# A weight block loaded earlier and multiplied ahead of a pair, at the DMA-bound start of an attention and expert kernel

## The chip, the cores and the metric

The kernel runs on 1 core of one Trainium2 chip. The metric is device microseconds (us) of one execution, as the median of several runs. A profile comes from one of these runs. Its span is about 1.8 us shorter than the run's device time. All times inside a profile count from the start of its span.

Engines: PE is TensorE (PEld its weight loads), DVE is VectorE, ACT is ScalarE, POOL is GpSimd, SP is SyncE.

## The reference, cut to what matters

```python
q, k, v: (batch 8, heads 8, sequence 576, head size 64), float32;  w_in: (512, 2048);  w_out: (2048, 512)

kv  = einsum('bhsd,bhse->bhde', k, v)              # linear attention: one 64x64 matrix per head
out = einsum('bhsd,bhde->bhse', q, kv)
out = out / sqrt(mean(out * out, axis=-1) + 1e-6) * g_norm
x   = out.transpose(0, 2, 1, 3).reshape(4608, 512)
h   = x @ w_in
g   = h * (1 / (1 + exp(-1.702 * h)))
result = g @ w_out                                 # (4608, 512) float32
```

## The kernel before

Batch by batch, the attention part makes x (transposed, float16), and the dense part multiplies it by w_in, gates it and multiplies it by w_out. The eight heads are handled as four pairs, and the 512 rows of w_in as four row blocks of 128. All transfers that matter here are issued by GpSimd one after another and cast from float32 to float16 on the way. The first batch has nothing to hide behind: its k, q, v and the whole of w_in arrive while PE already wants them.

The order of the transfers at the start:

```python
    for c in range(1, NPAIR):            # pairs 1 to 3 of batch 0
        for n in "qkv":
            early_load(n, 0, c, c + 1)
    load_w_in(0, 4, 0, 2)                # w_in: columns 0 to 3 (blocks of 128), row blocks 0 and 1
    load_w_in(0, 4, 2, KO)               # the same columns, row blocks 2 and 3
    load_w_in(4, GROUP)                  # columns 4 and 5, all rows
    load_w_in(GROUP, 10)
    load_w_in(10, FO)
```

PE's program for batch 0 up to the gates:

```python
    for _ in range(3):                   # warm-up: float32 products of zeros
        nc.tensor.matmul(idle_ps, zeros[:, 0:P], zeros, start=True, stop=True)
    a0.q(0)
    busy(2)                              # products that only keep PE busy
    a0.kv(0)
    ...                                  # [cut: pairs 1 and 2 in the same manner]
    a0.q(3)
    a0.kv(3)                             # waits for v of pair 3
    a0.sums(2)
    a0.apply(1)
    a0.out(3)
    a0.rs(2)
    a0.apply(2)
    busy(1)
    d0 = Hidden(0)
    for fo in range(4):                  # row block 0 (ko = 0) of columns 0 to 3
        d0.mm(0, fo, *((ps_h, "hT") if fo < 3 else (ps_a, "att")))
        if fo == 2:
            a0.ss(3)
            a0.apply(3)
    for ko in range(1, KO):
        for fo in range(4):
            d0.mm(ko, fo)
    for fo in range(4, GROUP):
        for ko in range(KO):
            d0.mm(ko, fo, ps_o, "o")
    for fo in range(GROUP):
        d0.gate(fo)
```

Afterwards column blocks 6 to 15 follow (four products and a gate each), then the 64 products with w_out. The work on batch 1 hangs on the numbers of those 64 steps (`at2(27, ...)` means after step 27).

Of the kernel before, what the change touches and what calls it, by code (L numbers as in the profile page):

```python
# [8 lines left out]
F32 = mybir.dt.float32  # L9
# [3 lines left out]
P = 128  # L13
# [3 lines left out]
def kernel(  # L17
# [10 lines left out]
    nc = tc.nc  # L28
# [119 lines left out]
    g_row = const.tile([1, D], F32)  # L148
    nc.scalar.dma_start(out=g_row, in_=g_norm.unsqueeze(0))
    nc.vector.memset(ident, 0.0)  # L150
    zeros = const.tile([P, SM], F32)
    nc.vector.memset(zeros, 0.0)
    nc.vector.memset(kvb[1], 0.0)
    nc.gpsimd.affine_select(  # L154
        out=ident,
# [19 lines left out]
    for c in range(1, NPAIR):  # L175
        for n in "qkv":
            early_load(n, 0, c, c + 1)
    load_w_in(0, 4, 0, 2)
    load_w_in(0, 4, 2, KO)
    load_w_in(4, GROUP)  # L180
    load_w_in(GROUP, 10)
    load_w_in(10, FO)

    nc.scalar.preload_act_table_set("natural_log_exp_and_others")
    nc.vector.memset(eps_t, EPS)
# [261 lines left out]
    def dense(t, units1, units2, group, deep, hid=None):  # L447
        hid = hid or Hidden(t)
        gT = hid.gT
        if group and t:  # L450
            order = [(ko, fo) for part in (range(4), range(4, group)) for ko in (0, 1) for fo in part]
            order += [(ko, fo) for ko in range(2, KO) for fo in range(group)]
            for ko, fo in order:
                pool = (ps_h, "hT") if fo < 3 else (ps_a, "att") if fo == 3 else (ps_o, "o")
                hid.mm(ko, fo, *pool)
            for fo in range(group):
                hid.gate(fo)
        for fo in range(FO):
            if fo >= group:
                for ko in range(KO):  # L460
                    hid.mm(ko, fo)
                hid.gate(fo)
            for u in units1.get(fo, ()):
                u()

        osb = osbs[t] = opool.tile([P, 4, DM], F32, name="osb", tag="osb")
        os = {}

        def project(mo, fo):
            if fo == 0:  # L470
                pool, tag = (ps_h, "hT") if deep and mo < 2 else (ps_o, "o")
                os[mo] = pool.tile([P, DM], F32, name="o", tag=tag)
            nc.tensor.matmul(  # L473
                os[mo],
                gT[:, fo, mo * P : (mo + 1) * P],
                w_out_sb[:, fo, :],
                start=(fo == 0),
                stop=(fo == FO - 1),
            )
            if fo == FO - 1:  # L480
                by_act = mo % 2 if deep or t == B else 0 < t < B - 1 and mo < 2
                copy = nc.scalar.copy if by_act else nc.vector.tensor_copy
                copy(osb[:, mo, :], os[mo])  # L483
                if t == B:
                    store_rest(mo, 0, DM)
                elif t in HALVED and mo % 2:
                    store(t, mo - 1, mo + 1)

        def store_rest(mo, n0, n1):
            for g in range(2):  # L490
                rows = out[(2 * mo + g) * S : (2 * mo + g + 1) * S, n0:n1]
                if 2 * mo + g < EARLY:
                    p0 = SM % PE_
                    rows = rows[bass.DynSlice(NJ * p0 + SM // PE_, R, step=NJ), :]
                else:
                    rows = rows[SM:S, :]
                queue = (nc.sync, nc.scalar)[g]
                queue.dma_start(out=rows, in_=osb[g * R : (g + 1) * R, mo, n0:n1])


        def project_last(mo):
            for i, (n0, n1) in enumerate(LAST):
                o = ps_a.tile([P, n1 - n0], F32, name="oh", tag="att")
                for fo in range(FO):
                    nc.tensor.matmul(  # L505
                        o,
                        gT[:, fo, mo * P : (mo + 1) * P],
                        w_out_sb[:, fo, n0:n1],
                        start=(fo == 0),
                        stop=(fo == FO - 1),  # L510
                    )
                copy = nc.vector.tensor_copy if i else nc.scalar.copy
                copy(osb[:, mo, n0:n1], o)
                store_rest(mo, n0, n1)

        if deep:
            steps = [(mo, 4 * i + k) for i in range(3) for mo in range(4) for k in range(4)]
            steps += [(mo, f + k) for f in (12, 14) for mo in range(2) for k in range(2)]
            steps += [(mo, 12 + k) for mo in (2, 3) for k in range(4)]
        else:  # L520
            steps = [(mo, fo) for mo in range(4 - (t == B)) for fo in range(FO)]
        for n, (mo, fo) in enumerate(steps):
            project(mo, fo)
            for u in units2.get(n, ()):
                u()
        if t == B:
            project_last(3)
        if t < EARLY:

            n = 0  # L530
            while n < SM:
                mo, j, p = n // P, n // PE_, n % PE_
                m = min((mo + 1) * P, (j + 1) * PE_) - n
                nc.sync.dma_start(
                    out=out[t * S : (t + 1) * S, :][bass.DynSlice(NJ * p + j, m, step=NJ), :],
                    in_=osb[n % P : n % P + m, mo, :],
                )
                n += m
        elif t < B and t not in HALVED:
            store(t, 0, J)  # L540
# [25 lines left out]
            )  # L566


    for _ in range(3):
        nc.tensor.matmul(idle_ps, zeros[:, 0:P], zeros, start=True, stop=True)  # L570
    a0.q(0)
    busy(2)
    a0.kv(0)
# [16 lines left out]
    a0.out(2)  # L590
    a0.rs(1)
    a0.q(3)
    a0.kv(3)
    a0.sums(2)
    a0.apply(1)
    a0.out(3)
    a0.rs(2)
    a0.apply(2)
    busy(1)
    d0 = Hidden(0)  # L600
    for fo in range(4):
        d0.mm(0, fo, *((ps_h, "hT") if fo < 3 else (ps_a, "att")))
        if fo == 2:
            a0.ss(3)
            a0.apply(3)
    for ko in range(1, KO):
        for fo in range(4):
            d0.mm(ko, fo)
    for fo in range(4, GROUP):
        for ko in range(KO):  # L610
            d0.mm(ko, fo, ps_o, "o")
    for fo in range(GROUP):
        d0.gate(fo)
    load_w_out(0, 4)
    early_load("q", 1, 0, NPAIR)
    load_w_out(4, 8)
    for c in (0, 2):
        load_half("k", 1, c, c + 2)
        load_half("v", 1, c, c + 2)
        if c == 0:  # L620
            load_w_out(8, 12)
        else:
            load_w_out(12, 14)
            load_w_out(14, FO)
    load_q(2, nc.gpsimd)

    nc.gpsimd.dma_start(out=g_all, in_=g_norm.unsqueeze(0).to_broadcast([P, D]))
# [8 lines left out]
    for t in range(NT):  # L636
# [12 lines left out]
        if t == 0:  # L649
            at1(7, of(0, "out", NPAIR))  # L650
            at2(4, setattr, a0, "ss_pool", Attention.ss_pool)
            at2(4, of(0, "ss", NPAIR, True))
            at2(4, of(0, "apply", NPAIR))
            at1(8, start, 1)
            for l in range(2):
                r = slice(l * PH, (l + 1) * PH)
                at1(8, nc.vector.memset, kpad[r, :, :, (1 - l) * D : (2 - l) * D], 0.0)
            for c in range(NPAIR):
                at1(12, of(1, "pack_q", c))
                at2(9 + 3 * c, of(1, "q", c))  # L660
                at2((21, 21, 33, 33)[c], of(1, "pack_k", c))
                at2((27, 28, 42, 43)[c], of(1, "kv", c))
                o = (32, 35, 50, 53)[c]
                at2(o, of(1, "out", c))
                if c == NPAIR - 1:
                    at2(46, load_kv, 2)
                at2((38, 46, 56, 59)[c], of(1, "ss", c))
                at2((38, 46, 56, 59)[c], of(1, "apply", c))
        elif b < B:
            if t == 1:  # L670
                at2(46, setattr, live[1], "ss_pool", Attention.ss_pool)
                at2(46, of(1, "out", NPAIR))
                at2(53, of(1, "ss", NPAIR))
                at2(53, of(1, "apply", NPAIR))
            f0 = 5 if t == 1 else 2
            at1(f0, cast_q, b)
            at1(f0, start, b)
            at1(f0, of(b, "transpose_q"))
            if t + 2 < B:
                at1(f0, load_q, t + 2)  # L680
                at1((10 if t == 1 else 9) + 4, load_kv, t + 2)
            for c in range(NPAIR):
                at1(f0, of(b, "pack_k", c))
                at1((10 if t == 1 else 9) + c, of(b, "kv", c))
            at2(6, nc.scalar.preload_act_table_set, "natural_log_exp_and_others")
            for j in range(J):
                at2((1, 4, 8, 11)[j], of(b, "rows", j))
            at2(7, of(b, "turn", 0))
            at2(16, of(b, "turn", 2))
            at2(27, of(b, "out", NPAIR))  # L690
            at2(36, of(b, "ss", NPAIR))
            at2(36, of(b, "apply", NPAIR))
# [31 lines left out]
```

## Time and profile before

| what | value |
|---|---|
| median of the runs beside the changed kernel | 286.96 us (286.64 to 287.28, 6 runs) |
| the profiled run | 286.75 us, span 285.0 us |
| v of pair 3 landed, its product starts | 12.88, 13.02 us |
| w_in row blocks 2 and 3 landed, first product with them | 16.53, 16.58 us |
| column blocks 6 and on start | 20.17 us |
| first product with w_out starts | 29.00 us |
| row block 1 of the dense part starts | 46.83 us |
| last product of the kernel starts | 281.32 us |

The last rows serve as milestones: the first product with w_out tells how the start went, row block 1 what was lost between, the last product the whole.

The page of this profile says three more things: how full DMA was in each fortieth of the span, how many instruction fetches ran, and what the chain that ended last is made of.

```profile
DMA  8999999999589356953798279925401410011022
...
q8 instruction: 13, 0.21, 0.3%
...
PE 93%; DMA 3%; POOL 3%; issue 0%; DVE 0%
```

The first row has a digit for every 7.1 us, in tenths of busy time of 16 engines: DMA is full for the first 70 us (8 or 9 tenths in each of the first ten). The second is queue, packets, MB and share: 13 packets of 16 KB in the queue that the profile calls instruction; the prediction takes them for the fetches of PE's program. They take 0.3% of DMA's time. The third: the end is set by PE for 93% of the span.

### The profile page before, as it was taken

How to read it: one execution, taken by the hardware profiler on the slowest of the kernel's cores; microseconds unless marked ns; L12 is line 12 of the kernel's file. 1: busy time of each engine (PE TensorE's matmuls, PEld its weight loads, DVE VectorE, ACT ScalarE, POOL GpSimd, SP SyncE). 2: the span in 40 equal slices, each digit the busy share in tenths (PEclk: the TensorE clock that was granted, in tenths of full speed). 3: DMA queues.
4: the chain of work that ended last, by engine and by line, in shares of the span. 5: the costliest groups of instructions: out<-in, count | busy, mean ns of one | idle time of the engine just before them, and what ended most of it. 6: DMA issues, size and time to landing. Idle time of an engine off the chain costs nothing.

```text
span 285.0 us, 4335 instructions
## 1 busy us (share of the span) xinstructions
PE 278.8 (98%) x1707; PEld 134.9 (47%) x1707; DVE 119.2 (42%) x231; ACT 156.2 (55%) x273; POOL 57.2 (20%) x82
## 2 busy tenths in 40 slices
PE   7899999999999999999999999999999999999995
PEld 3444554455445544554455445544454444444443
DVE  2650566527661657157713852286327400110001
ACT  2697439766575645574468536763666365016400
POOL 8931551111211121112011401130002100000000
PEclk9999999999999999999999999999999999999999
DMA  8999999999589356953798279925401410011022
GB/s 176 198 207 204 207 246 235 201 240 179 122 165 254 61 145 161 245 85 71 218 200 152 38 215 198 188 39 184 83 2 37 119 65 2 0 67 80 2 74 74
DMA packets 54070, 38.76 MB, mean 136 GB/s; under 512 B 31219, under 2 KB 50931, under 8 KB 53923
## 3 DMA queue, kind: packets, MB, share of 16 engines
q0 software_dynamic: 14960, 15.58, 33.5%
q1 hardware_dynamic: 38688, 22.39, 30.6%
q10 hardware_dynamic: 402, 0.52, 0.6%
q8 instruction: 13, 0.21, 0.3%
q14 instruction: 7, 0.05, 0.1%
HBM read 36.73 MB, written 9.44 MB: 162 GB/s over the span
## 4 chain that ended last, share of the span: by engine, by line
PE 93%; DMA 3%; POOL 3%; issue 0%; DVE 0%
PE hT L436 43%; PE o L473 42%; DMA w_in_sb<-in_moe_w_in_dram 3%; PE kvp L225 3%; PE outR L289 2%; PE oh L505 1%; POOL qraw L91 1%; POOL kraw L91 1%; POOL vbuf L91 1%; PE ss L337 1%; PE q L414 0%; PE outT L268 0%; PE outT L257 0%; POOL w_in_sb L168 0%; POOL ident L154 0%
## 5 line engine op out<-in xcount | busy, mean ns | idle before, releaser
L473 PE MATMUL o<-w_out_sb,gT 128*128 128x512 f16 x560 | 130.7, 379 | 0.0
L445 ACT ACTIVATE gT<-hT 128x512 f16<-128x512 f32 x144 | 84.7, 599 | 76.8 <-PE hT L436 76.5
L436 PE MATMUL hT<-xT,w_in_sb 128*128 128x512 f16 x512 | 116.5, 379 | 0.1
L436 PEld LDWEIGHTS <-w_in_sb 128*128 128x128 f16 x576 | 54.3, 98 | 63.1 <-DMA w_in_sb<-in_moe_w_in_dram 1.6
L473 PEld LDWEIGHTS <-gT 128*128 128x128 f16 x560 | 52.9, 98 | 56.4
L483 DVE COPY osb<-o 128x512 f32<-128x512 f32 x20 | 13.8, 690 | 62.3 <-PE o L473 62.3
L321 POOL TENSOR_TENSOR x<-xr,g_all 128x512 f16<-128x512 f32 x12 | 15.3, 1272 | 71.2 <-DVE xr L314 47.2
L216 DVE COPY kpad<-kraw 64x576 f16<-64x576 f16 x56 | 25.0, 446 | 1.7 <-DMA kraw<-in_k_dram 0.4
L300 DVE TENSOR_REDUCE sum<-sq 128x8 f32<-128x512 f16 x24 | 15.8, 679 | 19.9 <-ACT sq L297 19.9
L238 DVE CAST kvb<-kvp 64x128 f16<-64x128 f32 x28 | 8.1, 288 | 36.5 <-PE kvp L225 36.3
L314 DVE TENSOR_TENSOR xr<-outR,sum 128x512 f32<-128x512 f32 x24 | 15.5, 686 | 11.1 <-ACT sum L311 11.1
L112 POOL DMA_DIRECT2D kraw<-in_k_dram x16 | 10.0, 625 | 48.2 <-DVE kpad L216 42.3
L112 POOL DMA_DIRECT2D vbuf<-in_v_dram x16 | 9.7, 610 | 34.1 <-PE kvp L225 29.3
L321 DVE TENSOR_TENSOR x<-xr,g_all 128x512 f16<-128x512 f32 x12 | 15.2, 1267 | 0.7
L297 ACT ACTIVATE sq<-outR 128x512 f16<-128x512 f32 x24 | 13.6, 591 | 2.0 <-PE outR L289 1.6
L225 PEld LDWEIGHTS <-kpad 128*128 128x128 f16 x252 | 11.1, 98 | 6.5 <-DVE kpad L216 0.2
L436 PE MATMUL hT<-x_rem,w_in_sb 128*128 128x512 f16 x64 | 14.0, 379 | 0.0
L277 ACT ACTIVATE sq<-outT 128x512 f16<-128x512 f32 (+1 forms) x16 | 7.7, 481 | 11.0 <-PE outT L257 9.5
L483 ACT COPY osb<-o 128x512 f32<-128x512 f32 x15 | 8.7, 582 | 6.3 <-PE o L473 6.3
L310 ACT ACTIVATE sum<-sum,eps_t 128x16 f32<-128x16 f32 x12 | 3.7, 308 | 15.0 <-DVE sum L300 14.9
L225 PE MATMUL kvp<-vbuf,kpad 128*128 128x64 f16 x252 | 11.9, 193 | 0.0
L339 ACT ACTIVATE ln<-ss,eps_t 128x512 f32<-128x512 f32 (+1 forms) x16 | 9.4, 585 | 3.4 <-PE ss L337 3.4
(65 smaller groups left out, 140.7 us busy)
## 6 DMA issues: line engine op xcount, KB each, us to landing
qf<-in_q_dram SPq DMA_DIRECT2D x5, 1024.0 KB, 8.7
out_dram<-osb SPq DMA_DIRECT2D x10, 512.0 KB, 2.9
kraw<-in_k_dram POOLq DMA_DIRECT2D x12, 288.0 KB, 7.5
vbuf<-in_v_dram POOLq DMA_DIRECT2D x12, 288.0 KB, 5.4
w_out_sb<-in_moe_w_out_dram POOLq DMA_DIRECT2D x3, 512.0 KB, 14.8
out_dram<-osb SPq DMA_DIRECT2D x6, 192.0 KB, 5.6
qf<-in_q_dram POOLq DMA_DIRECT2D x1, 1024.0 KB, 12.2
out_dram<-osb SPq DMA_DIRECT2D x1, 1024.0 KB, 3.8
```

What stands on the lines that cost most here:

```text
L112: nc.gpsimd.dma_start(out=raw[n][l * PH : (l + 1) * PH, c0:c1, 0 : NH * D], in_=srcs[n][b].rearrange("(c l) (p j) d -> l p c (j d)", l=2, ...
L216: nc.vector.tensor_copy(out=kpad[r, c, :, l * D : (l + 1) * D], in_=kraw[r, c, 0 : NH * D].rearrange("p (j d) -> p j d", j=NH),)
L225: nc.tensor.matmul(self.kvp[:, c, :], kpad[:, c, j, :], vbuf[:, c, j * D : (j + 1) * D], start=(j == 0), stop=(j == NH - 1),)
L297: nc.scalar.activation(sq, t, AFT.Square)
L300: nc.vector.tensor_reduce(out=self.sum2[:, j % 2, :], in_=sq.rearrange("p (h d) -> p h d", h=H), op=ALU.add, axis=mybir.AxisListType.X,)
L314: nc.vector.tensor_mul(xr[:, i], self.o[j + i].rearrange("p (h d) -> p h d", h=H), s2[:, i, :].unsqueeze(2).to_broadcast([P, H, D]),)
L321: (nc.vector if i else nc.gpsimd).tensor_mul(self.x16[:, j + i, :].rearrange("p (h d) -> p h d", h=H), xr[:, i], g_all.unsqueeze(1).to_bro ...
L339: nc.scalar.activation(ln[:, 0:n], t[:, 0:n], AFT.Ln, bias=eps_t, scale=1.0 / D)
L436: nc.tensor.matmul(self.h[fo], w_in_sb[:, ko, fo * P : (fo + 1) * P], self.x[:, ko], start=(ko == 0), stop=(ko == KO - 1),)
L445: nc.scalar.activation(self.gT[:, fo, :], self.h[fo], AFT.Gelu_apprx_sigmoid)
L473: nc.tensor.matmul(os[mo], gT[:, fo, mo * P : (mo + 1) * P], w_out_sb[:, fo, :], start=(fo == 0), stop=(fo == FO - 1),)
L483: copy(osb[:, mo, :], os[mo])
```

## The change

The intent is to fill a hole. PE waits 0.76 us for v of pair 3. Row block 0 of w_in is moved ahead of k and v of that pair, so that PE can do its four products while v is on its way. Around this, the warm-up was made of smaller products, the rest of w_in was split in smaller transfers, and the transfers and steps of batch 1 were put in another order. The diff, cut to its core:

```diff
     for c in range(1, NPAIR):
         for n in "qkv":
             early_load(n, 0, c, c + 1)
-    load_w_in(0, 4, 0, 2)
+            if c == NPAIR - 1 and n == "q":
+                load_w_in(0, 4, 0, 1)
+    load_w_in(0, 4, 1, 2)
     load_w_in(0, 4, 2, KO)
     load_w_in(4, GROUP)
-    load_w_in(GROUP, 10)
-    load_w_in(10, FO)
+    load_w_in(GROUP, 8)                 # and (8, 10), (10, 13), (13, FO)
...
-            order = [(ko, fo) for part in (range(4), range(4, group)) for ko in (0, 1) for fo in part]
+            order = [(ko, fo) for part in ((0, 3, 1, 2), range(4, group)) for ko in (0, 1) for fo in part]
...
-    for _ in range(3):
-        nc.tensor.matmul(idle_ps, zeros[:, 0:P], zeros, start=True, stop=True)
+    for _ in range(64):
+        nc.tensor.matmul(
+            idle_ps[:, 0:D], kvb[1][:, 0, :], kvb[1][:, 0, 0:D], start=True, stop=True
+        )
+    busy(4)
...
     a0.q(3)
+    a0.apply(1)
+    d0 = Hidden(0)
+    d0.mm(0, 0)
+    a0.sums(2)
+    a0.rs(2)
+    d0.mm(0, 1)                         # and d0.mm(0, 2), d0.mm(0, 3)
     a0.kv(3)
-    a0.sums(2)
-    a0.apply(1)
+    a0.apply(2)
     a0.out(3)
...                                      # then row 1, row 2, rows 0-2 of columns 4 and 5, the last row of all six
-    for c in (0, 2):                    # k, v, w_out 8-11, k, v, w_out 12-13, w_out 14-15
-        load_half("k", 1, c, c + 2)
-        load_half("v", 1, c, c + 2)
...
+    load_half("k", 1, 0, 2)
+    load_w_out(8, 10)
+    load_w_out(10, 12)
+    load_half("v", 1, 0, 2)             # then k, v of the second half, w_out 12-13, 14-15
...
-                at2((27, 28, 42, 43)[c], of(1, "kv", c))
+                at2((36, 37, 46, 47)[c], of(1, "kv", c))
-                o = (32, 35, 50, 53)[c]
+                o = (41, 43, 52, 53)[c]
-                at2((38, 46, 56, 59)[c], of(1, "ss", c))
+                at2((45, 48, 56, 58)[c], of(1, "ss", c))
...                                      # batch 2's key products a block later, q of batch 3 loaded later
```

More of the change, by code (lines that the diff above doesn't have):

```diff
@@ L150 @@
     nc.vector.memset(ident, 0.0)
-    zeros = const.tile([P, SM], F32)
-    nc.vector.memset(zeros, 0.0)
     nc.vector.memset(kvb[1], 0.0)
@@ L177 @@
             early_load(n, 0, c, c + 1)
-    load_w_in(0, 4, 0, 2)
+            if c == NPAIR - 1 and n == "q":
+                load_w_in(0, 4, 0, 1)
+    load_w_in(0, 4, 1, 2)
     load_w_in(0, 4, 2, KO)
     load_w_in(4, GROUP)
-    load_w_in(GROUP, 10)
-    load_w_in(10, FO)
+    load_w_in(GROUP, 8)
+    load_w_in(8, 10)
+    load_w_in(10, 13)
+    load_w_in(13, FO)
     nc.scalar.preload_act_table_set("natural_log_exp_and_others")
@@ L592 @@
     a0.q(3)
+    a0.apply(1)
[4 more added lines that the diff above has]
+    d0.mm(0, 1)
+    d0.mm(0, 2)
+    d0.mm(0, 3, ps_a, "att")
     a0.kv(3)
-    a0.sums(2)
-    a0.apply(1)
+    a0.apply(2)
     a0.out(3)
-    a0.rs(2)
-    a0.apply(2)
-    busy(1)
-    d0 = Hidden(0)
     for fo in range(4):
-        d0.mm(0, fo, *((ps_h, "hT") if fo < 3 else (ps_a, "att")))
+        d0.mm(1, fo)
         if fo == 2:
@@ L605 @@
             a0.apply(3)
-    for ko in range(1, KO):
-        for fo in range(4):
-            d0.mm(ko, fo)
+    for fo in range(4):
+        d0.mm(2, fo)
     for fo in range(4, GROUP):
-        for ko in range(KO):
+        for ko in range(KO - 1):
             d0.mm(ko, fo, ps_o, "o")
+    for fo in range(GROUP):
+        d0.mm(KO - 1, fo)
     for fo in range(GROUP):
@@ L616 @@
     load_w_out(4, 8)
-    for c in (0, 2):
-        load_half("k", 1, c, c + 2)
-        load_half("v", 1, c, c + 2)
-        if c == 0:
-            load_w_out(8, 12)
-        else:
-            load_w_out(12, 14)
-            load_w_out(14, FO)
+    load_half("k", 1, 0, 2)
+    load_w_out(8, 10)
+    load_w_out(10, 12)
+    load_half("v", 1, 0, 2)
+    load_half("k", 1, 2, NPAIR)
+    load_half("v", 1, 2, NPAIR)
+    load_w_out(12, 14)
+    load_w_out(14, FO)
     load_q(2, nc.gpsimd)
@@ L660 @@
                 at2(9 + 3 * c, of(1, "q", c))
-                at2((21, 21, 33, 33)[c], of(1, "pack_k", c))
-                at2((27, 28, 42, 43)[c], of(1, "kv", c))
-                o = (32, 35, 50, 53)[c]
+                at2((21, 21, 38, 38)[c], of(1, "pack_k", c))
+                at2((36, 37, 46, 47)[c], of(1, "kv", c))
+                o = (41, 43, 52, 53)[c]
                 at2(o, of(1, "out", c))
                 if c == NPAIR - 1:
-                    at2(46, load_kv, 2)
-                at2((38, 46, 56, 59)[c], of(1, "ss", c))
-                at2((38, 46, 56, 59)[c], of(1, "apply", c))
+                    at2(48, load_kv, 2)
+                at2((45, 48, 56, 58)[c], of(1, "ss", c))
+                at2((48, 51, 56, 60)[c], of(1, "apply", c))
         elif b < B:
@@ L679 @@
             if t + 2 < B:
-                at1(f0, load_q, t + 2)
-                at1((10 if t == 1 else 9) + 4, load_kv, t + 2)
+                at1(12 if t == 1 else f0, load_q, t + 2)
+                at1((11 if t == 1 else 9) + 4, load_kv, t + 2)
             for c in range(NPAIR):
                 at1(f0, of(b, "pack_k", c))
-                at1((10 if t == 1 else 9) + c, of(b, "kv", c))
+                at1((11 if t == 1 else 9) + c, of(b, "kv", c))
             at2(6, nc.scalar.preload_act_table_set, "natural_log_exp_and_others")
```

## The prediction

> **What bounds the kernel now.** I read the page first. TensorE (PE) is busy for 98% of the span, so only what PE does not do usefully can be won. I then split the span into stretches, because a share over the whole span hides where PE is short of work.
>
> ```profile
> PE 278.8 (98%) x1707; PEld 134.9 (47%) x1707; DVE 119.2 (42%) x231; ACT 156.2 (55%) x273; POOL 57.2 (20%) x82
> ...
> 6.53:12.40 5.87, 5.46 (x98) 1.00 1.30 198
> 12.40:14.24 1.84, 1.15 (x17) 1.00 1.23 195
> 14.24:20.17 5.93, 5.79 (x27) 1.00 1.27 206
> 20.17:28.95 8.78, 8.78 (x45) 1.00 1.24 206
> 28.95:46.83 17.88, 17.88 (x135) 1.00 1.21 229
> ```
>
> The rows are stretch, PE busy, clock, DMA share, GB/s. PE has idle time only before 20.17 us, and DMA runs at about 200 GB/s (counted at the destination, float16) all the way. As matmul ends are modelled, I judged PE by start-to-start spacing: in a full stream a 512-column matmul starts every 216 ns. From 24 us to the end spacing exceeds that by over 40 ns in two places only, 85 ns before the second key/value product of batch 1 (36.75 us) and 130 ns in the first products of row block 1 (47.39 us). So everything to be won lies before 24 us, plus 0.2 us.
>
> The chain of waits says what sets the end there:
>
> ```profile
> 8.01 0.72 POOL w_in_sb L168
> 8.73 7.80 DMA w_in_sb<-in_moe_w_in_dram
> 16.53 0.05 issue
> 16.58 5.48 PE hT L436 x24
> 22.06 0.12 PE outT L268 x4
> 22.17 6.99 PE hT L436 x32
> ```
>
> The second w_in transfer (rows 2 and 3 of the first four column blocks) lands at 16.53 us, and from there PE runs to the end. The waits of PE and its weight loads name the same:
>
> ```profile
> PE kv L374 <- DMA vbuf<-in_v_dram: 0.6, 1, 0.6
> ...
> PEld L436 <- DMA w_in_sb<-in_moe_w_in_dram: 1.6, 4, 0.6
> ```
>
> The start is a race with a saturated DMA queue, so the losses (spacing over 216 ns) before 24 us fall to it: 0.76 us for v of pair 3 (13.02), 0.30 us for w_in rows 2-3 (16.58), 0.07 us for the last w_in (23.81). 0.13 us at 17.58 is VectorE's last x (16.78 to 17.53).
>
> [...] Once started, a 128x64 product with its own weights takes 29 ns per step in this trace (nine L225 in one run)[...]. [...] for the transfer that gated the chain 15 engines were done by 15.45 us and the sixteenth at 16.53. That engine was late after an instruction fetch:
>
> ```profile
> q0 software_dynamic: 450, 0.29, 131.3%
> q8 instruction: 1, 0.02, 3.7%
> ```
>
> This is the queue view of 14 to 15.5 us: one 16 KB fetch. 13 such fetches come about 240 TensorE instructions apart, so I take them for PE's program.
>
> **The change part by part.**
> *Warm-up.* Removed: three float32 products (six records, 1.54 to 6.54 us) and the zeros memset, 0.48 us of VectorE. Added: 64 products of 64 columns plus four of 512. They can start at about 1.3 us instead of 1.54. [...] The first q transposes then start between 6.05 (q cast done at 6.01) and 6.5. But the first kv waits for the v cast, 6.92 to 7.59 us, which waits for its transfer; it stays at 7.64. Worth 0 us.
> *w_in row 0 between q and k of pair 3.* It moves 128 KB ahead. At 200 KB/us that is 0.65 us, so row 0 lands near 12.1, v of pair 3 at 12.88 + 0.65 = 13.5, row 1 at 14.2 as before. In the hole (PE waited 12.2 to 13.02) go the sum of pair 2 and four row-0 products, 5 x 0.216 = 1.08 us; they begin when x of pair 0 is written (12.56). I get the four products at 12.65 to 13.8, kv of pair 3 at 13.8 to 14.05, its output at about 14.6 (VectorE applies pair 1 first, to 14.2), row 1 from 14.8.
> *What this wins.* Before, 16 of the 24 grouped products come after 16.58: 16 x 0.216 = 3.46, plus the 0.13 gap, gives 20.17. Afterwards the same 16 still need rows 2-3, and blocks 4-5 need the next transfer, landed 17.49 before. Neither moves: the bytes ahead of them are the same. At 17.49 at least 12 products remain (six for blocks 4-5, six of the last row): 17.5 + 12 x 0.216 = 20.1. If the late engine recovers (its fellows were done at 16.78), rows 2-3 finish at about 17.0, then 12 products end at 19.6. So 0.07 to 0.57 us is won here, not the 0.76 of the filled wait.
> *Split of the rest of w_in.* Blocks 6-7, 8-9, 10-12, 13-15 separately: block 10 no longer waits for the last landing at 23.76. It is needed at about 23.7 and lands near 21.9. Worth 0.07 us and keeps the gain usable.
> *w_out, k, v of batch 1 reordered.* w_out 8-11 lands near 35.8 instead of 37.43 (first used at 37.67: slack 0.24). v of the first half goes from 34.66 to about 37.2, so its product moves from steps 27-28 to 36-37, at about 38.5. The last w_out piece stays at 42.7, used at 43.59: 0.9 us of slack. The 85 ns gap at 36.75 should go.
> *Batch 2 and 3.* Key steps one block later give 0.86 us to v of batch 2 (landed 55.97, used 56.45). q of batch 3 later takes traffic from the batch-2 transpose (landed 61.68, used 62.25). PE waits for neither now, so these are worth 0 us by themselves: they keep slack for an earlier PE.
> *Order (0,3,1,2).* 0.13 us at 47.39.
> Sum: 0.07 to 0.57 + 0.07 + 0.085 + 0.13 = 0.35 to 0.85 us. I take 0.6.
>
> **The rivals.** (a) *The wait only moves:* DMA still sets 20.17 us and PE stands before rows 2-3 or blocks 4-5 instead of v. For: same bytes, share of 1.27. It leaves 0.3 us. (b) *The fetch strikes earlier:* PE's program has 133 more instructions ahead of the first q; the first fetch (14.4 us, after 245 PE instructions) would move to about 10 us, the second (35.4 us) to about 28. The first would then delay v of pair 2 by up to 0.7 us and shift the whole chain. For: the spacing of the fetches. Against: PE had 0.8 us to wait anyway. My table with that delay again ends near 20.1 us: a gain of 0.3 us, in a worse case 0. (c) *ScalarE becomes the bound:* the last row's products come at once, then six gates at a spacing of 0.53 us; the ninth block's buffer is free 3.98 us after the first last-row product, and PE asks for it after 3.99. A late table load (1.28 us) could cost 0.2. (d) *A large win of over 1 us:* needs the whole start to run ahead of the DMA; slack of 0.24 to 0.9 us at later landings speaks against it.
>
> **Range and chances.** 287.08 - 0.6 = 286.45 us. Runs of the kernel before spread over 0.64 us, and one row of late engines is worth 0.5, so the range is 285.7 to 287.1. Two per cent is 5.7 us; even all spacing lost between 6.5 and 24 us is 3.6 us, so faster by 2% gets 0.015. Slower would need a new wait of 5.7 us: 0.015.
>
> **What would show it.** Right: PE's wait for v of pair 3 gone from the waits; the second-block stream starting by 20.1 us or earlier; both later gaps gone; PE's last matmul 0.3 to 0.9 us earlier. Step by step wrong: row 0 landing after 12.9 us; kv of pair 3 after 14.3 us; first kv later than 7.7 us [...]; waits for w_out, k or v in 33 to 44 us or for the transpose near 62 us. The size would be wrong if the fetch at 14 us was not PE's, or if the sixteenth engine is not late in the new order: then more is won than I say.

Marked passages of this text are cut. They stated PE's clock at its start and the working of DMA as rules, which no trace here shows; the cuts in three expectations below are of the same kind. Two terms of one sum went with them: from a start at 1.3 us the new warm-up came to an end at 6.5 us, an estimate that rested on such a rule. The gain doesn't hang on it: the warm-up is worth 0 us there, and the sum of 0.35 to 0.85 us stands whole.

What the traces show: in the kernel after, the 64 small products of the warm-up start 53 ns apart (1.28 to 4.68 us) and the four large ones 0.41 to 0.43 us apart, where later small ones with their own weights start 29 ns apart and large ones 216 ns. In the kernel before, five records of the old warm-up took 1061 or 1221 ns, started 0.85 us apart but for the first, and the last took 637. The clock records of the two traces begin at 6.05 (before) and 7.18 us (after), so they don't say at which clock the warm-up ran. That a transfer put ahead delays one behind it shows in a4_extra: 144 KB more put row block 0 back by 0.59 us.

## The result, and the profile after

| | before | after |
|---|---|---|
| median, lowest to highest, 6 runs each | 286.96 us, 286.64 to 287.28 | 286.97 us, 286.44 to 287.17 |
| ratio after / before, 95% interval | | 0.9998, 0.9985 to 1.0011 |

A ratio here is the mean time of one kernel's fast runs over that of the other's in the same rounds, so it isn't quite the ratio of the medians that are quoted. The change is worth nothing within 0.15%; the 0.6 us that I had expected (0.2%) lies outside the interval.

The profiled run of the kernel after was the slowest of its six (287.17 us), the one of the kernel before was a little under its median. Between these two traces lie 0.43 us (last product at 281.32 and at 281.75), which the medians don't confirm. I use the pair to see where time was won and lost, not for the size of the whole.

The page of the kernel after:

```profile
PE 278.8 (98%) x1768; PEld 136.9 (48%) x1768; DVE 119.2 (42%) x230; ACT 156.0 (55%) x273; POOL 59.5 (21%) x86
...
q8 instruction: 14, 0.23, 0.3%
...
PE 83%; DMA 13%; POOL 2%; issue 0%; DVE 0%
```

PE is as busy as it was, with 61 more products and one more fetch. But the chain that sets the end is now DMA for 13% of the span instead of 3%. Which transfers those are, the chain in order of time tells (start, duration, what; the DMA rows between issue and landing):

```profile
6.34 6.84 DMA w_in_sb<-in_moe_w_in_dram
13.18 0.28 issue
13.46 8.55 DMA w_in_sb<-in_moe_w_in_dram
22.02 0.29 issue
22.30 14.60 DMA w_out_sb<-in_moe_w_out_dram
36.91 0.29 issue
37.20 6.60 DMA w_out_sb<-in_moe_w_out_dram
43.80 0.04 issue
43.84 0.38 PE o L475
```

Before, PE ran free of DMA from 16.58 us to the end. Now a transfer of w_out that lands at 43.80 us holds the product that starts at 43.84. In this trace GpSimd issues its transfers in order, and each only after the one eight before it has landed (here the issues at 13.46, 22.30 and 37.20 after the landings at 13.18, 22.02 and 36.91), so the chain goes back from that landing through the earlier ones to row block 0 at 13.18. The waits of PE after 8 us (what waited, for whom: us, times, longest) name the start again:

```profile
PE hT L438 <- DMA w_in_sb<-in_moe_w_in_dram: 0.8, 1, 0.8
PE outT L259 <- DVE kvb L383: 0.4, 1, 0.4
```

The wait for v is gone, as intended. In its place stands a wait of the same size for row block 0 itself. The second row is the output of pair 3, which waits for VectorE to write that pair's matrix. The timeline of PE shows it (start, duration, instruction, in brackets the idle time before it and what ended it):

```profile
11.98 0.45 PE L393 MATMUL q<-ident,qraw 96*64 96x96 f16 x12
13.22 0.39 PE L438 MATMUL hT<-xT,w_in_sb 128*128 128x512 f16 x1 [0.79 <-DMA w_in_sb<-in_moe_w_in_dram]
...
14.41 0.38 PE L376 MATMUL kv<-vbuf,kraw 96*64 96x64 f16 x12
15.20 0.39 PE L259 MATMUL outT<-qT,kvb 128*128 128x512 f16 x1 [0.42 <-DVE kvb L383]
```

Why was row block 0 late? The trace has sixteen landings for each of these transfers; I read them as its 16 engines, one each. Fifteen of the sixteen engines of row block 0 were done at 12.14 us, which is what I had expected of all (12.1). The sixteenth was done at 13.18. In 11 to 12.5 us the queue view of the kernel before and then of the kernel after has:

```profile
DMA packets 385, 0.30 MB, mean 199 GB/s; under 512 B 31, under 2 KB 385, under 8 KB 385
```

```profile
DMA packets 305, 0.24 MB, mean 159 GB/s; under 512 B 27, under 2 KB 304, under 8 KB 304
...
q8 instruction: 1, 0.02, 4.0%
```

After, one instruction fetch runs in these 1.5 us, from 11.13 us on, a single packet of 948 ns. 4.0% of 16 engines' 1.5 us is that packet. (The lower rate, 159 against 199 GB/s, is not the fetch's alone: a1_warm12 has 171 GB/s in this window without a fetch, and its row block 0 is in time. What tells is the one late engine. The trace doesn't name a packet's engine; that the fetch and the lateness share one is read from the times.) In the kernel before the first fetch came at 14.40. The second moved as well, from 35.38 to 24.22 us. All packets of this queue are of 16 KB. Here row block 0 landed 1.04 us after its other fifteen engines were done, and PE was idle for 0.79 us before it.

The stretches that the prediction showed (us, PE busy, PEld, DVE, ACT, POOL, PE clock, DMA share, GB/s):

```profile
12.40:14.24 1.84, 1.05 (x7) 0.41 (x5) 1.30 (x3) 1.41 (x4) 0.78 (x2) 1.00 1.26 200
14.24:20.17 5.93, 5.47 (x37) 2.42 (x36) 2.81 (x4) 4.96 (x8) 4.18 (x6) 1.00 1.40 198
28.95:46.83 17.88, 17.64 (x132) 8.87 (x131) 10.12 (x24) 8.92 (x15) 9.01 (x14) 1.00 1.20 229
```

In 12.40 to 14.24 PE does less than before (1.05 against 1.15 us), and in 28.95 to 46.83 it is idle at times, where it was full before (17.64 against 17.88). With start-to-start spacing over the 216 ns of a 512-column product, the pair of traces comes to this ledger (+ is a loss against before):

| where | before | after | difference, us |
|---|---|---|---|
| up to the first w_out product | 29.00 | 28.98 | -0.02 |
| gap at 36.75 us (key/value of batch 1) | 0.085 | none | -0.085 |
| gap at 38.41 us: v of batch 1, first half, landed 38.27 | none | 0.30 | +0.30 |
| gap at 43.84 us: last w_out, landed 43.80 | none | 0.27 | +0.27 |
| gap at 46.08 us: sum after step 58 | none | 0.09 | +0.09 |
| gap at 47.39 us (first products of row block 1) | 0.13 | none | -0.13 |
| sum | | | +0.43 |

The sum is the difference of the last products, 281.75 - 281.32 = 0.43.

### The profile page after: what moved, and what is told of

Same layout as the page of the kernel before. It is cut to its first block, busy times and chain, and to the rows that moved or that the text cites. A ratio compares the mean times of both kernels' runs of the same rounds, so it can differ in the third digit from the quotient of the medians.

```text
span 285.4 us, 4458 instructions
## 1 busy us (share of the span) xinstructions
PE 278.8 (98%) x1768; PEld 136.9 (48%) x1768; DVE 119.2 (42%) x230; ACT 156.0 (55%) x273; POOL 59.5 (21%) x86
## 4 chain that ended last, share of the span: by engine, by line
PE 83%; DMA 13%; POOL 2%; issue 0%; DVE 0%
PE hT L438 39%; PE o L475 38%; DMA w_out_sb<-in_moe_w_out_dram 7%; DMA w_in_sb<-in_moe_w_in_dram 5%; PE kvp L227 2%; PE outR L291 2%; PE oh L507 1%; POOL qraw L91 1%; PE ss L339 0%; POOL kraw L91 0%; POOL vbuf L91 0%; PE outT L270 0%; PE outT L259 0%; DVE osb L515 0%; POOL ident L152 0%
## 5 line engine op out<-in xcount | busy, mean ns | idle before, releaser
L485 DVE COPY osb<-o 128x512 f32<-128x512 f32 x20 | 13.8, 691 | 62.4 <-PE o L475 62.4
```

Of the source, the lines that this page charges most:

```text
L485: copy(osb[:, mo, :], os[mo])
```

## The experiments

**My theory (T)** after this reading: the longer warm-up program pulls the fetch onto row block 0; that costs about 1 us at the start, and the fetch at 24.22 costs 0.57 us more at 38 and 44 us. **Rival B:** the start is bound by bytes, as the prediction said; row blocks 2-3 and columns 4-5 would hold PE at 20.1 us even if row block 0 came in time. **Rival S:** the smaller pieces of w_in are what made the landings late. **Rival O:** the new order of batch 1 is what loses, by itself.

Twelve runs, of eleven kernels, were made in four calls, each on another chip. The runs of the kernel before had medians of 286.86, 286.90, 286.92 and 286.78 us, so compare kernels by their ratios. The milestones below come from one profile of each kernel.

| kernel | row block 0 landed | first w_out product | row block 1 | last product | median, lowest to highest (runs) | ratio to before, 95% |
|---|---|---|---|---|---|---|
| before | 14.19 (with row 1) | 29.00 | 46.83 | 281.32 | see above | |
| after | 13.18 | 28.98 | 47.38 | 281.75 | 286.97 (6) | 0.9998 |
| a1_warm12 | 12.25 | 29.12 | 47.10 | 281.47 | 286.89, 286.76 to 287.22 (5) | 1.0002, 0.9990 to 1.0014 |
| b1_warm64 | 14.72 (with row 1) | 29.52 | 47.34 | 281.86 | 288.51, 287.30 to 289.01 (6) | 1.0049, 1.0032 to 1.0066 |
| b3_warm64_fill | 14.63 (with row 1) | 29.49 | 47.33 | 281.82 | 287.39, 287.19 to 287.57 (5) | 1.0012, 1.0000 to 1.0024 |
| b2_row0 | 12.07 | 28.85 | 47.16 | 281.69 | 287.17, 286.86 to 287.26 (6) | 1.0004, 0.9989 to 1.0018 |
| a2_nosplit | 13.06 | 29.26 | 47.24 | 281.61 | 287.05, 286.49 to 289.23 (6) | 1.0016, 0.9991 to 1.0040 |
| a3_oldorder | 12.88 | 28.68 | 46.60 | 280.97 | 286.72, 286.42 to 286.83 (5) | 0.9996, 0.9983 to 1.0009 |
| a4_extra | 13.77 | 29.66 | 47.64 | 282.01 | 287.43, 287.32 to 287.58 (4) | 1.0015, 1.0002 to 1.0028 |
| a5_less | 13.45 | 29.25 | 47.23 | 281.60 | 286.94, 286.53 to 290.04 (6) | 1.0016, 0.9981 to 1.0050 |
| a7_warm86 | 12.66 | 28.79 | 47.64 | 282.41 | 287.58, 286.94 to 289.53 (6) | 1.0025, 0.9997 to 1.0054 |
| c1_best | 12.66 | 28.77 | 47.75 | 282.79 | 289.48, 288.21 to 292.36 (6) | 1.0095, 1.0058 to 1.0132 |
| a6_step60 | 12.14 | 29.02 | 46.76 | 281.26 | 286.57, 286.29 to 286.82 (5) | 0.9989, 0.9975 to 1.0002 |

### a1_warm12: the change with a warm-up of few instructions

Twelve products of 512 columns in place of 64 small and four large ones. The transfers are the same, so only PE's program gets shorter. By the spacings of the warm-up in the kernel after, 53 ns and 0.41 to 0.43 us, eight large products take as long as 64 small ones, 3.4 us; this is an estimate.

```diff
-    for _ in range(64):
-        nc.tensor.matmul(idle_ps[:, 0:D], kvb[1][:, 0, :], kvb[1][:, 0, 0:D], start=True, stop=True)
-    busy(4)
+    busy(12)
```

> The changed kernel with its 64 small warm-up products replaced by eight more 512-column ones: [...] 112 TensorE instructions fewer. Fetch theory: the first 16 KB instruction fetch moves from 11.13 us to between 14 and 18 us, the second from 24.2 to 33 us or later; w_in row 0 lands by 12.3 us instead of 13.18, PE does not wait for it (0.94 us now), and the last w_out piece lands by 43.2 us instead of 43.80; 0.3 to 0.7 us faster than the changed kernel. Byte theory (the transfers bound it whatever the fetch does): fetch moves, but blocks 6 on still start at 20.1 us and the time stays within 0.15 us.

The fetches went back to 14.80 and 35.26 us. Row block 0 landed at 12.25, and its products started at 12.49, when VectorE had x ready, not DMA. So the fetch, and with it the lateness of row block 0, follow PE's instruction count: this part of T is shown. Yet the time did not change. Its timeline tells why:

```profile
12.49 0.38 PE L438 MATMUL hT<-xT,w_in_sb 128*128 128x512 f16 x1 [0.19 <-DVE xT L353]
...
15.88 0.38 PE L438 MATMUL hT<-xT,w_in_sb 128*128 128x512 f16 x1
16.91 1.04 PE L438 MATMUL hT<-xT,w_in_sb 128*128 128x512 f16 x4 [0.65 <-DMA w_in_sb<-in_moe_w_in_dram]
```

PE is 0.73 us earlier at row block 0, and then waits for row blocks 2-3, which landed at 16.86 us: the fetch now falls on their way, as it did in the kernel before. Fifteen of its engines were done at 15.67, so this lateness too is one engine's. From 16.91 the 16 products that are left end at 16.91 + 16 x 0.216 = 20.37. So PE does stand before row blocks 2-3 when row block 0 comes in time, as rival B says, but because the fetch is on their way, not by bytes alone. At 38 and 44 us the gaps are gone, as T said. The late second fetch need not be the reason: a2_nosplit and a5_less have it at 24.24 and 24.27 us and no such gaps either. But a wait of 0.24 us stands after step 58 at 45.81 us, where the kernel after had 0.09. The products of that step on PE, then ScalarE's row that ends at the same moment:

```profile
45.13 0.59 PE L475 MATMUL o<-w_out_sb,gT 128*128 128x512 f16 x2
45.81 0.38 PE L339 MATMUL ss<-sq,ones 128*128 128x512 f16 x1
```

```profile
45.17 0.59 ACT L485 COPY osb<-o 128x512 f32<-128x512 f32 x1
```

The sum at step 58 starts when ScalarE's copy of a finished output ends (45.17 + 0.59 = 45.76): I read it as the buffer that both use. In the kernel after PE came 0.27 us later, and so waited less there. Waits in series hide one another.

### b1_warm64, b1_again and b3_warm64_fill: the warm-up alone

The kernel before with the new warm-up only; once more (one profiled run, no timing); and with five idle products put ahead of the key/value product of pair 3.

```diff
-    for _ in range(3):
-        nc.tensor.matmul(idle_ps, zeros[:, 0:P], zeros, start=True, stop=True)
+    for _ in range(64):
+        nc.tensor.matmul(idle_ps[:, 0:D], kvb[1][:, 0, :], kvb[1][:, 0, 0:D], start=True, stop=True)
+    busy(4)
...
     a0.q(3)
+    busy(5)                             # b3_warm64_fill alone
     a0.kv(3)
```

> The kernel before with the new warm-up alone (about 130 TensorE instructions more). Fetch theory: first fetch near 11 us, v of pair 3 lands at 13.5 to 13.9 us instead of 12.88 and PE waits 1.3 to 1.7 us for it, second fetch near 24 us; 0.3 to 0.8 us slower than before. Byte theory: same as before within 0.15 us.

> The kernel before with the new warm-up alone, once more, to see a run of its slow kind (four of six had a mean granted clock of 0.994 and took 1.2 to 1.7 us more). Clock theory: in such a run about 3.4 us of the start (0.006 x 285 x 2) run at half clock, after the 1.2 us wait for v of pair 3 near 13 us, and the loss of 1.5 us sits there. Other theory: the half clock lies at the end of the span and the loss elsewhere.

> The same with five idle 512-column products (1.08 us) put where PE waits for v of pair 3. Clock theory: no run with a granted clock of 0.994, all within 0.3 us of 287.3, so about 1.2 us faster than the new warm-up without them. If the slow runs have another cause: again about 288.5 in most runs.

With no other part of the change, the first fetch moved to 10.88 us and v of pair 3 landed at 13.48 instead of 12.88:

```profile
12.10 0.45 PE L389 MATMUL q<-ident,qraw 96*64 96x96 f16 x12
13.62 0.38 PE L372 MATMUL kv<-vbuf,kraw 96*64 96x64 f16 x12 [1.07 <-DMA vbuf<-in_v_dram]
```

The first w_out product starts 0.52 us later than before, the last product 0.54 us later. So the warm-up isn't worth 0 us but costs half a microsecond. In the whole change such a loss counts against whatever the row block gains.

I had not expected the rest. Four of the six runs took 288.50 to 289.01 us with a mean granted clock of 0.994 (they are under 1.5% longer than the fastest, and the ratio of 1.0049 holds them). The other two, at 0.999 and 1.0, took 287.30 and 287.52. The clock records of the traces know only 1.0 and 0.5 (in the kernel before 1.0 from 6.05 us and 0.5 from 285.95 us on, after the span). A mean of 0.998 can be the very end of the span: in a4_extra the record falls to 0.5 at 284.57 us, 1.1 us before its end. If the rest of a run is at 1.0, a mean of 0.994 is 0.006 x 285 x 2 = 3.4 us at 0.5, an estimate. My guess was that the wait of 1.07 us for v has to do with it, and b3_warm64_fill puts products there. In it no run of five is below 0.998, and they take 287.19 to 287.57 us, with the same late start (29.49). The kernel before had one such run in 42 (288.16 us at 0.994), the whole change none in six. b1_again was a run with full clock (287.2 us), and the profiled run of b1_warm64 has 1.00 in every stretch from 5.83 to 16.07 us, so no trace holds a drop at the start. That the clock falls in or just after this wait stays a guess from the clocks of the runs and from b3; it was not shown. Nor is the chip ruled out as the cause: b1_warm64 ran on one chip, b1_again and b3 on another, and there no run dropped.

### b2_row0: the row block alone

The kernel before with the early row block and the new order of its products, and nothing else: warm-up, the other transfers and batch 1 as before.

```diff
+            if c == NPAIR - 1 and n == "q":
+                load_w_in(0, 4, 0, 1)
-    load_w_in(0, 4, 0, 2)
+    load_w_in(0, 4, 1, 2)
...                                      # and PE's order from a0.q(3) to the gates, as in the change
```

> The kernel before with row 0 between q and k of pair 3 and the product order of the change, old warm-up and all else old. Fetch theory: fetch at 14 to 15 us, row 0 lands near 12.2, its products start by 12.6, the wait moves to w_in rows 2-3 (landing near 16.8, PE waits about 0.8 us), blocks 6 on start at 20.1 to 20.4: same as before within 0.3 us. If row 0 were worth what it fills (0.76 us): 0.5 us or more faster.

The fetches stayed at 14.48 and 35.06 us, row block 0 landed at 12.07, as the prediction had it (12.1), row blocks 2-3 at 16.59. Columns 6 and on started at 20.10 us; the prediction said 20.1. This is the start that I had sized, and it gains 0.07 us. The first w_out product is 0.15 us earlier, and then the gain is lost to a transfer behind it. The waits of PE name it:

```profile
PE o L475 <- DMA w_out_sb<-in_moe_w_out_dram: 0.3, 1, 0.3
PE hT L438 <- DMA w_in_sb<-in_moe_w_in_dram: 0.2, 1, 0.2
```

w_out 8-11 landed at 37.97 instead of 37.43 us and cost 0.485 us of spacing at 38.01. Fifteen of its engines were done at 37.14 us. The fetch at 35.06 had come just before: the transfer that landed last ahead of it had its sixteenth engine 0.32 us behind the fifteenth (34.39, 34.07), this one 0.83 us. So this trace doesn't show that the row block needs the new order of batch 1, and a3_oldorder, with the old one, has no such gap: its w_out 8-11 landed at 37.39.

### a3_oldorder: the change with the old order of batch 1

Rival O: transfers and steps of batch 1 as before, all else as in the change.

```diff
-    load_half("k", 1, 0, 2)             # and so on, as in the change
+    for c in (0, 2):                    # k, v, w_out 8-11, k, v, w_out 12-13, w_out 14-15
...
-                at2((36, 37, 46, 47)[c], of(1, "kv", c))
+                at2((27, 28, 42, 43)[c], of(1, "kv", c))
...                                      # and the other steps of batch 1
```

> The changed kernel with batch 1's transfers and its steps in the old order. If late landings are what takes the gain: w_out 8-11 lands near 38.5 us, after its first use at 37.0 to 37.6, so PE waits 0.5 to 1 us there and the kernel is 0.3 to 0.8 us slower than the changed one. If the new order itself costs time (its waits of 0.30 us at 38.41 and 0.27 at 43.84): 0.3 to 0.5 us faster.

No gap of 0.30 or 0.27 us is left in 30 to 47 us, only 0.086 at 36.43 and 0.079 at 37.43. Its row block 0 was somewhat luckier (12.88 us, with a fetch at 10.84; columns 4-5 landed at 17.25) and its first w_out product 0.30 us earlier. Its second fetch, at 23.72, cost the last w_out transfer nothing (landed at 42.84). Its profiled run, 286.42 us, was the fastest of its five, so its trace flatters it: the median is 286.72, and the ratio's interval holds 1. The old order is not worse than the new one; whether it is better by 0.1 or 0.2 us these runs can't tell.

### a2_nosplit: w_in's rest in two transfers, as before

Rival S.

```diff
-    load_w_in(GROUP, 8)                 # and (8, 10), (10, 13), (13, FO)
+    load_w_in(GROUP, 10)
+    load_w_in(10, FO)
```

> The changed kernel with the rest of w_in in two transfers again (blocks 6-9, 10-15). Descriptor theory [...]: the last w_in lands about 0.25 us earlier than 23.93, the last w_out piece near 43.55 instead of 43.80, the 0.27 us wait at 43.84 goes; 0.1 to 0.3 us faster. Fetch theory: no change.

Row block 0 was as late (13.06 us), so S doesn't explain the start. Here four engines were late, from 12.70 on, the other twelve by 12.09; one fetch packet doesn't explain four, and that stays open. The last w_in transfer landed at 24.03, not 0.25 us before the 23.93 of the kernel after, as the expectation's first theory had it. The last w_out transfer landed at 42.98 instead of 43.80 us, but not because of the pieces: fifteen engines were done at 42.94 here and at 42.90 in the kernel after. The 0.82 us are the sixteenth engine's. A gap of 0.07 us at 24.07 came back, which is the one that the split was to remove. One run of six had a clock of 0.986 and took 289.23 us; the other five have a mean of 286.93. As a whole: no difference.

### a4_extra and a5_less: bytes ahead, bytes fewer

To see how the time follows bytes at the start, a4_extra loads 144 KB that nobody uses ahead of row block 0. a5_less leaves 128 KB out behind it (row block 3 of columns 0 to 3 is taken from row block 2, so its result is wrong, relative error 0.35).

```diff
+                nc.gpsimd.dma_start(out=spare[0:PE_]..., in_=early_src("k", 0, 3, 4))     # a4_extra
                 load_w_in(0, 4, 0, 1)
...
-    load_w_in(0, 4, 2, KO)
+    load_w_in(0, 4, 2, 3)               # a5_less; its products read row block 2 for 3
```

> The changed kernel with one more 144 KB transfer (k of pair 3 a second time, to a spare buffer) ahead of w_in row 0. Byte theory: every later landing 0.7 us later, blocks 6 on start at 20.9 us, later waits at 38.4 and 43.8 grow to 0.9 us: 0.7 to 1.2 us slower than the changed kernel. If latency or the fetch, not bytes, sets the start: under 0.2 us.

> The changed kernel without the first four blocks of w_in row 3 (128 KB fewer; wrong result on purpose, row 2 is read in their place). Byte theory: landings after it 0.65 us earlier, blocks 6 on start 0.3 to 0.6 us earlier (what is left is VectorE's last x at 18.8 us), waits at 38.4 and 43.8 gone: 0.5 to 0.9 us faster than the changed kernel. Otherwise: within 0.2 us.

a4_extra moved row block 0 by 0.59 us and the first w_out product by 0.68 us, near the 0.72 us that 144 KB take at 200 GB/s. But the last product moved by only 0.26 us and the median by 0.46 us, because the last w_out transfer landed only 0.19 us later and PE no longer waited long for it. a5_less gained nothing: 286.94 against 286.97 us (one run of its six, with a clock of 0.988, took 290.04). Its row block 0 happened to be later (13.45, fetch at 11.41), so PE started its products 0.28 us later than in the kernel after, and did the rest in the same 6.94 us up to column 6 (13.50 to 20.44, against 13.22 to 20.17). So in the kernel after bytes *behind* row block 0 don't bind and bytes *ahead* of it do.

Here three limits meet, and they come out nearly alike. With row block 0 late, column 6 starts 6.94 us after its first product: 13.22 to 20.17 in the kernel after, 13.50 to 20.44 in a5_less. With row block 0 early and the fetch on row blocks 2-3 (a1_warm12, b2_row0), 16 products follow those, from 16.91 and 16.64 us on: 20.37 and 20.10. With the fetch on neither, or row block 0 less late, columns 4-5 hold PE, and 12 products follow: 17.44 + 12 x 0.216 = 20.03 in a7_warm86 (measured 20.04), 17.30 + 2.59 = 19.89 in a3_oldorder (19.90). All end near 20.1 us. In a7_warm86 the weight loads show that third wait:

```profile
17.43 1.63 PEld L438 LDWEIGHTS <-w_in_sb 128*128 128x128 f16 x9 [0.48 <-DMA w_in_sb<-in_moe_w_in_dram]
```

### a7_warm86: the fetch moved once more

If T is right, other counts of warm-up instructions must put the fetch elsewhere. By the same spacings as in a1_warm12, 86 small products and one large take about 0.1 us less than the 64 and four, an estimate, and are 19 products more.

```diff
-    for _ in range(64):
+    for _ in range(86):
...
-    busy(4)
+    busy(1)
```

> The changed kernel with 86 small warm-up products and one large in place of 64 and four: [...] 38 TensorE instructions more. Fetch theory (the fetch delays the transfer then under way, and the row-0 products start a chain of fixed length, 6.94 us to blocks 6 on): the first fetch moves to 10.0 to 10.5 us and delays q of pair 3, which has slack; row 0 lands at 12.3 to 12.7 instead of 13.18, blocks 6 on start at 19.4 to 19.8 instead of 20.16. The time moves by less, 0 to 0.3 us faster, as the last w_out piece still lands near 43.5. Other theory: row 0 still lands after 13 us and nothing moves.

The fetch moved to 9.83 us and hit q of pair 3 (landed 12.18 us, 1.02 later than in the kernel after); the second went to 21.09. Row block 0 landed at 12.66, as I had expected. Column 6 started at 20.04 us, not at 19.4 to 19.8: columns 4-5 had landed only at 17.39. The first w_out product came at 28.79, 0.19 us earlier than in the kernel after. But v of batch 1 (0.45 us at 38.37), the last w_out transfer (0.59 at 44.11) and v of batch 2 (0.38 at 58.39) all held PE. The w_in transfer that was under way at the second fetch landed at 23.16, with fifteen engines done at 22.02, and v of batch 1 still had one engine behind (38.23, fifteen at 37.40). One run of six had a clock of 0.986 and took 289.53 us. The place of the fetch is shown again; as a remedy it failed.

### c1_best: an attempt at a better kernel

a7_warm86 with v of batch 1's second half behind the last w_out transfer, and its products and sums later.

```diff
-    load_half("v", 1, 2, NPAIR)
     load_w_out(12, 14)
     load_w_out(14, FO)
+    load_half("v", 1, 2, NPAIR)
...
-                at2((36, 37, 46, 47)[c], of(1, "kv", c))
+                at2((36, 37, 50, 51)[c], of(1, "kv", c))
...                                      # out at 55 and 57, sums at 60 and 62
```

> The same, with v of batch 1's second half after the last w_out pieces, its products at steps 50 and 51, and the last two sums at steps 60 and 62 (after ScalarE's copy of the second result block). If the later landings and step 58 took the gain: the last w_out lands near 42.3, no wait over 0.1 us after 30 us, and the time is 0.3 to 0.8 us under before. If not: within 0.2 us of before.

It is the slowest of all. The last w_out transfer came at 41.54 us, over 2 us earlier, and its wait is gone. (The second fetch, again at 21.10, left the transfer under way at 22.02 instead of 23.16, so what it costs differs from run to run.) But the products of batch 1, pressed into the last steps, wait by the profile for VectorE and ScalarE: gaps of 0.29, 0.76, 0.18 and 0.67 us at 41.96, 43.37, 45.15 and 49.06. At the second of these v, now behind w_out, had itself landed only at 43.23. Three of its six runs also had a clock of 0.988 to 0.994.

### a6_step60: the short warm-up, and the last sum two steps later

The two changes that the traces recommended: a1_warm12, and the sum that waited at step 58 at step 60.

```diff
+    busy(12)                            # in place of the 64 small and four large products
...
-                at2((45, 48, 56, 58)[c], of(1, "ss", c))
+                at2((45, 48, 56, 60)[c], of(1, "ss", c))
```

> The changed kernel with twelve large warm-up products (as a1_warm12) and the last sum of batch 1 at step 60 instead of 58, after ScalarE's copy of the second result block is done. If that copy is what PE waits for at 45.8 us (0.24 us in a1_warm12): the gap goes, no other gap over 0.1 us between 18 and 60 us, and the time is 0.15 to 0.3 us under a1_warm12, near 286.65. If the wait has another cause: it moves with the step and the time stays at 286.9.

The wait is gone, as PE's timeline shows:

```profile
45.03 1.03 PE L475 MATMUL o<-w_out_sb,gT 128*128 128x512 f16 x4
45.89 0.38 PE L339 MATMUL ss<-sq,ones 128*128 128x512 f16 x1
46.11 0.81 PE L475 MATMUL o<-w_out_sb,gT 128*128 128x512 f16 x3
46.76 1.15 PE L438 MATMUL hT<-xT,w_in_sb 128*128 128x512 f16 x4
```

45.03 + 4 x 0.216 = 45.89: the sum follows without a gap, and row block 1 starts at 46.76 us, 0.34 earlier than in a1_warm12. The gap in row block 1 came back for it, 0.13 us at 47.53, so the last product is 0.21 us earlier. The median is 286.57 us against 286.78 of the kernel before in the same rounds, the best of all kernels here, and the interval of its ratio, 0.9975 to 1.0002, just touches 1. A gain of 0.2 us is likely and not proven.

## Why the prediction was right and wrong

*Within 2%, in the range:* right. 286.97 us lies in 285.7 to 287.1, near its upper end. The expected gain of 0.6 us did not come, and the lower bound of 0.35 us on the sum didn't hold either. That the time lies in the range is partly luck: the range allowed for the spread of the runs and for one row of late engines, and what the sum had wrong happened to come to no more than that. And at 2% of 286.96, 5.7 us, "the same" was all but sure for any change of this size. Two slips in the text change nothing: 287.08 - 0.6 is 286.48, and ahead of the first q the traces record 139 TensorE instructions against 15, 124 more and not 133.

*"It stays at 7.64. Worth 0 us."* Right for the first key/value product (7.67 us), wrong for the warm-up. Its instructions, not its time, were the cost: 0.54 us at the last product with the warm-up alone (b1_warm64).

*"Row 0 lands near 12.1."* **This is the step that failed first.** It landed at 13.18, with 15 engines at 12.14. The number held where the fetch stayed in its old place (12.07 in b2_row0, 12.25 in a1_warm12). Rival (b) had the fetch moving to about 10 us and named v of pair 2 as its victim; it moved to 11.13 and struck the very block that the change brings forward. I had left it out of the table that gave the 12.1, though I had written it down as a rival.

*"I get the four products at 12.65 to 13.8, kv of pair 3 at 13.8 to 14.05."* 13.22 to 14.4 and 14.41 in the trace, by that lateness. b2_row0 started them at 12.67.

*"Neither moves ... 20.1."* Right, and for the kernel after by another way than I thought: not rows 2-3 (16.06) or columns 4-5 (17.39) held PE there but a fixed chain of 6.94 us behind row block 0. Where row block 0 came in time, rows 2-3 held PE (a1_warm12, b2_row0) or columns 4-5 did (a7_warm86, by the prediction's own sum of 12 products), as rival (a) said. The optimistic end, 19.6, would have needed columns 4-5 at about 17.0; the earliest landing in any run was 17.20 (a5_less).

*"0.07 for the last w_in."* The gap at 23.81 went, and one of 0.064 us at 22.94 came. It is in the place of rival (c), the ninth block that asks for its buffer just as it becomes free; that the buffer is what held it I did not test.

*"The 85 ns gap at 36.75 should go", "0.13 us at 47.39."* Both went. These two terms of the sum are right.

*"v of the first half goes to about 37.2", "the last w_out piece stays at 42.7 ... 0.9 us of slack."* **The second step that failed, and the larger one in this trace:** they landed at 38.27 and 43.80, about 1.1 us late each, and cost 0.30 and 0.27 us. I had the second fetch at about 28 us; it came at 24.22, before either transfer. In a1_warm12, whose transfers are the same and whose second fetch is at 35.26, the last piece landed at 43.22 and neither gap is there. The prediction gave landings without asking which of the sixteen engines is last: fifteen had the last piece at 42.90, near its 42.7.

*The sum of 0.35 to 0.85 us* was therefore wrong in two terms and short of one. The start gave 0.02 in place of 0.14 to 0.64 (the start and the split together). The later gaps gave 0.215 as said, and 0.57 for late landings and 0.09 for the sum at step 58 were missing. That wait was in the kernel's steps from the first and could have been read from the diff: the sum moved from step 59 to 58.

How much of the lateness at 38 and 44 us is the fetch's, and how much that of smaller pieces and order? The landings by engine tell. In the kernel after, the last w_in transfer had its sixteenth engine 0.17 us behind the fifteenth (23.93, 23.76). The next transfer, under way at the fetch of 24.22, had it 1.16 us behind (27.60, 26.44), and the last w_out transfer still 0.90 (43.80, 42.90). Fifteen engines were no later than in a2_nosplit (42.94) or a1_warm12 (42.90). So the pieces cost nothing at 44 us, and the order at most 0.2 (fifteen at 42.69 in a3_oldorder); one engine cost the rest.

But an early second fetch does not always do this: with one at 23.4 to 24.3 us, the last w_out transfer landed at 42.63 (b1_warm64), 42.57 (b1_again), 42.83 (b3_warm64_fill), 42.84 (a3_oldorder) and 42.98 us (a2_nosplit). I read it so that the fetch costs where it falls on the engine that is behind already. The traces don't name the engines, so this stays open, and so does whether the other five runs of the kernel after lost the 0.57 us: the trace is of the slowest of them.

## What to carry to other kernels

At a start where DMA is full, look for the instruction fetches in the queue view before you add instructions to an engine. Filler products of few columns look free in time, and here they still brought the next fetch forward (from 14.40 to 11.13 us), and the transfer that it hit was late by about a microsecond (13.18 us, its fifteen other engines 12.14). Up to the first fetch the windows count 239 matmuls and weight loads in the kernel before (six records fewer than the prediction's 245), 255 in a1_warm12, 292 in a7_warm86 and 303 in the kernel after, so its place has to be read from a trace, not counted. The lateness can last: from 27.60 to 43.80 us in the kernel after, each of these transfers had its sixteenth engine 0.8 to 1.2 us behind the fifteenth. Before you fill a wait, ask what the next transfer would hold anyway; here three limits put column 6 between 19.9 and 20.4 us, so removing one was worth nothing. And when transfers are put in a new order, check each one's slack against one such microsecond, not against its landing in a single trace.
